# A retuned order for an attention and MoE kernel, a last chunk with one more float32 pair, and the softmax guard on another engine

## The chip, the cores and the metric

The kernel runs on one core of a Trainium2 chip. A core has five engines with a queue each, and every queue runs its instructions strictly in order: TensorE (PE; the profile shows its weight loads apart as PEld), VectorE (DVE), ScalarE (ACT), GpSimd (POOL) and SyncE (SP), which here only issues DMA transfers. Engines wait for each other by semaphores. The metric is the device time of the whole program in microseconds (us), the median of several runs.

## The reference

Two steps follow each other. The first is attention through 32 inducing points, done twice; the second is a feed-forward layer with a quadratic gate.

```
def mab(q, kv):
    s = scale * (q @ kv.transpose(0, 2, 1))
    s = s - s.max(-1, keepdims=True)
    a = np.exp(s)
    a /= a.sum(-1, keepdims=True) + 1e-09
    return a @ kv
h = mab(I, x)            # I [32, 128], x [4, 12480, 128] -> h [4, 32, 128]
attn = mab(x, h)         # [4, 12480, 128] = 49920 tokens
u = attn @ w_in          # [49920, 2048]
g = where(u >= 1, u, where(u <= -1, 0, (u + 1)**2 / 4))
out = g @ w_out          # [49920, 128]
```

The 1e-9 added to the softmax's sum is called the guard below.

## The kernel before

The four batches are cut into 26 chunks of 480 tokens each, 104 in all; four neighbouring chunks make a group (the last group of a batch has two). The feed-forward layer never forms the attention's output: it multiplies the attention weights (32 numbers per token) by hw = h @ w_in, so the hidden layer of a chunk comes from one matmul per 128 hidden columns. A chunk is worked in eight pairs k = 0 to 7, each of 256 hidden columns, that is two PSUM banks of 480 columns.

One pair goes like this. Two hidden matmuls on TensorE (L943) fill two of seven banks. ACT computes relu(u + 1) from the banks (L951), in one instruction of 960 columns where both banks are neighbours and taken together, else in two of 480, and squares it with a factor (L937). DVE takes the minimum of that and max(u, 1) (L956, 960 or twice 480 columns), which gives the gate g in a buffer w and frees the banks. Then g meets w_out. In the pairs of SPLIT = (0, 1, 3, 4, 6, 7) g is rounded to hi, a cast by DVE (L979), ACT (L976) or POOL (L974), and POOL forms lo = g - hi (L982); six matmuls (L1008) in the faster format add hi x w_lo, hi x w_hi and lo x w_hi. In the other pairs two float32 matmuls use g and w_f as they are (each shows as two records). The eight pairs add up in one bank; DVE transposes it (L1020) and four stores (L1024) write it out.

Beside the chunks of batch b run the steps that make ready what comes later. The summary of batch b + 1 (first attention) goes group by group: loads of x (L498), transposes on TensorE (L507), scores (L547), maximum (L552), exponential on ACT (L564), transposed weights copied to eN (L588, L596), weighted sums (L604, "the gather", copied by L611); then one chain over the groups: total maximum (L645 to L661), a rescaling exponential on ACT (L664), sums and reciprocals (L667 to L675), h (L678, L686, L690), and hw from h and w_in (L712, L717, L720, spread by DMAs, L732). The second attention of a group (`attend`) takes scores (L757), softmax steps on DVE, ACT and POOL (the guard on POOL, L783, the reciprocal on DVE, L786, the normalization on POOL, L789), and copies into aT by DMA (L823). For the very first chunk a shorter path (`attend_first`, L845 to L892) is taken.

At the start nothing can overlap: batch 0's summary, the weights (w_in and w_out are loaded and turned by L398 to L434 into exactly split parts; L463, L470 and L472 make the tiles w_f, w_lo and w_hi) and the first attention run before the first hidden matmul. In TensorE's gaps there the kernel puts warm-up matmuls of the identity (L1035, `keep_on`).

The order of all instructions is computed in Python when the kernel is built. Each step is added to a planner with an engine, a cost, a lag after which others can use its result, and a due time; a list scheduler then fixes the order of every engine. The due times come from a table DUE: one number per pair and kind of step (h hidden, r relu, s square, t the minimum, hi per engine, lo, p, pl and pf the matmuls), and further entries for the summary, the weights (wi, wc, wo, oc) and the start (names ending in 0). Five more numbers steer it: LONE (a price for taking two banks singly), WAIT, RETILE, RAW and WARM. So a number in this table changes an order and nothing else.

Of the kernel before, what the change touches and what calls it, by code (L numbers as in the profile page):

```python
# [9 lines left out]
F32 = mybir.dt.float32  # L10
# [8 lines left out]
AHEAD = []  # L19
# [28 lines left out]
    "end": [-102700],  # L48
# [15 lines left out]
LONE = {"r": 8650, "t": 0}  # L64
# [3 lines left out]
WAIT = 181850  # L68

RAW = dict(DVE=205, ACT=130, POOL=100, PE=100, SP=0)  # L70
RETILE = 100
# [174 lines left out]
def attn_moe(  # L246
# [127 lines left out]
    def load_f32(src, when, due, dst=None, after=None):  # L374
# [61 lines left out]
        f = add("SP", 1120, 3000, when, fetch, [after], [raw])  # L436
# [18 lines left out]
    def load_out(k, when, due):  # L455
        src = w_out[k * WS : (k + 1) * WS].rearrange("(p t) d -> p t d", t=2)
        whole, parted = any(k not in t for t in [SPLIT, *AHEAD]), any(k in t for t in [SPLIT, *AHEAD])
# [22 lines left out]
    def summarize(b, begin, pace, end):  # L480
# [610 lines left out]
```

## Time and profile before

| what | value |
|---|---|
| median of three runs | 1732.78 us (1732.76, 1732.78, 1734.93) |
| the profiled execution's own time | 1733.12 us |
| its span, from first to last instruction | 1731.2 us |
| mean granted TensorE clock | 0.996 |
| first hidden matmul (L943), first relu (L951) | 66.60, 67.12 us |
| end of the last matmul, of the span | 1725.28, 1731.2 us |
| busy: PE, DVE, ACT, POOL | 1702.3, 1625.2, 1662.0, 1619.2 us |

Busy time of PE counts pipelined matmuls with modelled ends. "w L951 <- PE banks L943" reads: ACT's instruction of line 951 that writes w waited for TensorE's of line 943 that writes banks. In rows by shape, "x976 | 531.6, 609" are instructions, busy us and mean ns of one, then follow the idle time ahead of them and what ended it. A PE instruction in float32 counts as two records.

### The profile page before, as it was taken

What the parts mean: (1) busy time and instruction counts of PE and PEld (TensorE: products, weight loads), DVE (VectorE), ACT (ScalarE), POOL (GpSimd) and SP (SyncE); (2) the same over time, 40 slices, a digit from 0 to 9 for tenths busy, and PEclk for the clock granted to TensorE, in tenths of its full rate; (3) what the DMA queues carried; (4) which work ended last, traced back from release to release, by engine and by line L of the source; (5) the groups of instructions that cost most, each with busy time, mean ns of one, the idle gap of its engine ahead of it and who ended that gap; (6) DMA issues with size and microseconds to landing.
All of it is one profiled execution on the core that took longest, in us unless ns stands there. A gap on an engine that the chain in (4) does not pass through costs nothing.

```text
span 1731.2 us, 26016 instructions
## 1 busy us (share of the span) xinstructions
PE 1702.3 (98%) x8100; PEld 1242.9 (72%) x8100; DVE 1625.2 (94%) x2123; ACT 1662.0 (96%) x2453; POOL 1619.2 (94%) x879
## 2 busy tenths in 40 slices
PE   7999999999999999999999999999999999999998
PEld 5777777777777777767767777777777777777776
DVE  4899999999999999999999999999999999999997
ACT  5699999999999999999999999999999999999997
POOL 1599999999899999999989999999999999999998
PEclk9899999999999999999999999999999999999999
DMA  8543334233343243342143333232212111111111
GB/s 210 136 75 69 67 60 81 48 63 62 62 83 60 51 79 65 64 80 56 36 85 63 73 65 71 51 66 52 44 27 59 35 31 29 34 35 35 34 30 18
DMA packets 427948, 105.74 MB, mean 61 GB/s; under 512 B 370562, under 2 KB 421218, under 8 KB 427810
## 3 DMA queue, kind: packets, MB, share of 16 engines
q1 hardware_dynamic: 427714, 103.96, 30.7%
q8 instruction: 64, 1.05, 0.3%
q14 instruction: 74, 0.61, 0.1%
q10 hardware_dynamic: 96, 0.13, 0.0%
HBM read 48.94 MB, written 25.56 MB: 43 GB/s over the span
## 4 chain that ended last, share of the span: by engine, by line
PE 72%; ACT 9%; DVE 8%; issue 4%; POOL 3%; DMA 2%; SPq 1%; POOLq 0%; DVEq 0%; ACTq 0%
PE banks L1008 49%; PE banks L943 16%; ACT w L951 5%; DVE w L956 4%; ACT w L937 4%; POOL lo L982 3%; DVE hi L979 2%; PE banks L604 1%; PE banks L757 1%; PE banks L547 1%; PE banks L507 1%; DMA xr<-in_x 1%; DVE oT L1020 1%; PE banks L588 1%; PE banks L1035 1%
## 5 line engine op out<-in xcount | busy, mean ns | idle before, releaser
L982 POOL TENSOR_TENSOR lo<-w,hi 128x960 fp32r<-128x960 f32 x624 | 1399.7, 2276 | 40.7 <-DVE hi L979 21.3
L956 DVE SCALAR_TENSOR_TENSOR w<-banks,w 128x480 f32<-128x480 f32 (+1 forms) x1158 | 957.0, 863 | 36.6 <-ACT w L937 30.2
L951 ACT ACTIVATE w<-banks 128x480 f32<-128x480 f32 (+1 forms) x1320 | 841.9, 711 | 16.6 <-PE banks L943 15.1
L937 ACT ACTIVATE w<-w 128x960 f32<-128x960 f32 x832 | 843.2, 1046 | 3.2
L943 PE MATMUL banks<-aT,hw 128*128 128x480 f32 x1664 | 592.3, 425 | 5.3 <-DVE w L956 3.1
L1008 PE MATMUL banks<-hi,w_lo 128*128 128x480 f32 x1248 | 520.6, 417 | 4.7 <-DVE oT L1020 3.6
L979 DVE TENSOR_REDUCE hi<-w 128x960 fp32r<-128x960 f32 x410 | 466.1, 1142 | 19.3 <-PE banks L1008 1.3
L1008 PE MATMUL banks<-hi,w_hi 128*128 128x480 f32 x1248 | 473.4, 379 | 0.0
L943 PEld LDWEIGHTS banks<-aT,hw 128*128 128x128 f32 x1664 | 305.6, 188 | 158.6 <-DVE w L956 74.0
L1008 PE MATMUL banks<-lo,w_hi 128*128 128x480 f32 x1248 | 398.8, 396 | 0.7 <-POOL lo L982 0.5
L1008 PE MATMUL banks<-w,w_f 128*128 128x480 f32 x832 | 395.3, 565 | 0.0
L1008 PEld LDWEIGHTS banks<-hi,w_lo 128*128 128x128 f32 x1248 | 234.8, 188 | 87.8 <-issue 26.4
L1008 PEld LDWEIGHTS banks<-lo,w_hi 128*128 128x128 f32 x1248 | 230.7, 188 | 73.6 <-issue 23.1
L1008 PEld LDWEIGHTS banks<-hi,w_hi 128*128 128x128 f32 x1248 | 234.7, 188 | 53.0 <-issue 22.0
L1008 PEld LDWEIGHTS banks<-w,w_f 128*128 128x128 f32 x832 | 156.1, 189 | 46.8 <-issue 27.2
L974 POOL TENSOR_SCALAR hi<-w 128x960 fp32r<-128x960 f32 x143 | 142.9, 1006 | 5.1 <-PE banks L943 1.2
L1020 DVE STREAM_TRANSPOSE oT<-banks 128x480 f32<-128x480 f32 x104 | 70.2, 675 | 9.9 <-PE banks L1008 9.5
L976 ACT CAST hi<-w 128x960 fp32r<-128x960 f32 x71 | 71.5, 1008 | 6.3 <-DVE w L956 2.3
L528 DVE STREAM_TRANSPOSE xT<-xr 128x480 f32<-128x480 f32 x78 | 51.2, 660 | 1.8 <-DMA xr<-in_x 1.8
L434 POOL TENSOR_TENSOR w_in_sb<-hi,lo 128x256 f32<-128x256 f32 x8 | 6.9, 862 | 39.8 <-DVE hi L423 39.8
L800 POOL TENSOR_TENSOR a<-a,ahi 128x480 fp32r<-128x480 f32 (+1 forms) x28 | 34.6, 1235 | 0.0
L552 DVE TENSOR_REDUCE mg<-banks 128x1 f32<-128x480 f32 (+1 forms) x28 | 18.1, 647 | 16.0 <-PE banks L547 16.0
(107 smaller groups left out, 609.7 us busy)
## 6 DMA issues: line engine op xcount, KB each, us to landing
out<-oT SPq DMA_DIRECT2D x416, 60.0 KB, 2.2
xn<-in_x SPq DMA_DIRECT2D x91, 240.0 KB, 4.4
xr<-in_x SPq DMA_DIRECT2D x312, 60.0 KB, 2.5
aT<-ahi SPq DMA_DIRECT2D x206, 60.0 KB, 2.0
aT<-a SPq DMA_DIRECT2D x206, 60.0 KB, 2.0
w<-in_moe_w_in SPq DMA_DIRECT2D x8, 256.0 KB, 3.6
w<-in_moe_w_out SPq DMA_DIRECT2D x8, 256.0 KB, 5.2
hw<-hy SPq DMA_DIRECT2D x32, 64.0 KB, 2.0
```

What stands on the lines that cost most here:

```text
L528: nc.vector.transpose(make(xT[b, c]), xr.tile.rearrange("c n i -> c (n i)"))
L800: nc.gpsimd.tensor_sub(a.tile.bitcast(F32R)[:rows], a.tile[:rows], a_hi.tile[:rows].bitcast(F32))
L937: nc.scalar.activation(w.tile, w.tile, AF.Square, scale=0.5)
L943: nc.tensor.matmul(make(h)[:, :CW], hw[b][ft // 4].tile[:, ft % 4 * P : (ft % 4 + 1) * P], aT[b, c].tile, start=True, stop=True,)
L951: each(of, i, hs_, w, lambda to, h: nc.scalar.activation(to, h, AF.Relu, bias=1.0))
L956: lambda to, h: nc.vector.scalar_tensor_tensor(to, h, 1.0, to, op0=ALU.max, op1=ALU.min),
L974: nc.gpsimd.tensor_scalar(make(hi), w.tile, 1.0, 0.0, op0=ALU.mult, op1=ALU.add)
L976: nc.scalar.copy(make(hi), w.tile)
L979: nc.vector.tensor_reduce(make(hi), w.tile.unsqueeze(3), axis=AX.X, op=ALU.max)
L982: nc.gpsimd.tensor_sub(make(lo), w.tile, hi.tile.bitcast(F32))
L1008: nc.tensor.matmul(acc.tile[:, :CW], wt[k][:, i, :], g.tile[:, i, :], start=first, stop=(acc.parts == 0),)
L1020: nc.vector.transpose(make(oT).rearrange("c n i -> c (n i)"), acc.tile[:, :CW])
```

## The change

Four edits, and a table.

1. The table DUE is replaced as a whole. Two new kinds stand in it: G and W give the time at which each of the seven groups of a summary begins, and at which its gather is due; before, both were equally spaced. LONE, WAIT and RETILE have other values, and the planner is told other costs and lags for the loads at the start (the weights' 1080 and 5500 ns for 1120 and 3000; x of batch 0: 1000 and 5800 for 1080 and 3000).
2. In the very last chunk the pairs of END = (0, 1, 3, 4, 6) are split; pair 7 stays in float32, which takes one more weight tile w_f7 (one ACT copy at the start), two more float32 matmuls and six fewer of the others, and one hi and one lo less.
3. The last chunk's four stores are issued by SP and ACT in turn, not all by SP.
4. The guard moves from POOL (L783 before) to DVE, right ahead of the reciprocal (L791, L792 after).

A branch for hi and lo taken from the banks is added too; its table KEPT is empty, so no pair takes it.

```diff
-AHEAD = []
+END = (0, 1, 3, 4, 6)
+KEPT = {}
...
-LONE = {"r": 8650, "t": 0}
+LONE = {"r": 20200, "t": 4100}
-WAIT = 181850
+WAIT = 173500
-RETILE = 100
+RETILE = 120
...
 DUE = {
...
+    "G": [-3000, 51380, 98260, 151290, 202220, 254700, 307980],
+    "W": [61076, 111606, 164336, 213966, 267096, 319426, 370406],
...
-        f = add("SP", 1120, 3000, when, fetch, [after], [raw])
+        f = add("SP", 1080, 5500, when, fetch, [after], [raw])
...
-                    "SP", 700 if b else 1080, 3000, at(due, "x") if b else at(0, "x0", c),
+                    "SP", 700 if b else 1000, 3000 if b else 5800, at(due, "x") if b else at(0, "x0", c),
...
         for g in range(NG):
-            load(g, begin + g * pace, pace * 0.2)
-            s = score(g, begin + (g + 0.85) * pace)
+            base = at(begin, "G", g)
+            load(g, base, pace * 0.2)
+            s = score(g, base + 0.85 * pace)
             if last:
-                gather(g - 1, begin + (g + 0.2) * pace, last)
+                gather(g - 1, at(begin, "W", g - 1), last)
...
-        def guard():
-            nc.gpsimd.tensor_scalar(sm[:rows], sm[:rows], 1e-9, None, op0=ALU.add)
-
         def invert():
+            nc.vector.tensor_scalar(sm[:rows], sm[:rows], 1e-9, None, op0=ALU.add)
             nc.vector.reciprocal(sm[:rows], sm[:rows])
...
-        o = add("POOL", 339, 440, AT[6], guard, [o], [s2])
-        o = add("DVE", 165, 300, AT[6], invert, [o], [s2])
+        o = add("DVE", 290, 430, AT[6], invert, [o], [s2])
...
+            split = k in (END if (b, c) == (B - 1, NCH - 1) else SPLIT)
+            kept = split and k in KEPT
...
-            if k in [*AHEAD, SPLIT][min(b * NCH + c, len(AHEAD))]:
+            if kept:
...
+            elif split:
...
-        def store(k):
+        def store(k, queue):
             ks = slice(k * M, (k + 1) * M)
-            nc.sync.dma_start(o_cols[b, c][:, :, ks], oT.tile[ks])
+            queue.dma_start(o_cols[b, c][:, :, ks], oT.tile[ks])
...
         for k in range(Q):
-            add("SP", 640, 3000, at(due, "o") + 5000, lambda k=k: store(k), [f], [oT])
+            engine = "ACT" if (b, c) == (B - 1, NCH - 1) and k % 2 else "SP"
+            add(engine, 640, 3000, at(due, "o") + 5000,
+                lambda k=k, queue=nc.scalar if engine == "ACT" else nc.sync: store(k, queue), [f], [oT])
```

Every line number after the change is some 5 to 8 higher in the first attention and some 40 higher at the end of a chunk (L951 becomes L958, L982 becomes L1024, L1035 becomes L1079).

What it does to the order, counted over the program: ACT has 1343 relu instructions for 1320 and 74 casts of hi for 71, and three eN copies fewer; DVE has 1199 instructions of L956's kind for 1158, 406 hi copies for 410, three eN copies more and the 28 guards; POOL has 623 lo for 624 and no guard; the warm-ups on TensorE fall from 81 to 65, and behind the first hidden matmul from 45 to 19.

Three places. The first is ACT around the rescaling exponential of batch 0 (L664 before, L672 after; mg and nm are the groups' and the total maximum; L398 and L405 are the first step on a loaded weight; w_ numbers below 200 are loads). Before:

```order
L611 COPY hs_72<-banks_64 128x128
L596 COPY eN_161_823<-banks_64 96x4x64
L598 COPY eN_161_823<-banks_64 96x64
L398 ACTIVATE hi_162_830<-w_150_768 128x256
L664 ACTIVATE banks_64<-mg_70,nm_0_83 128x7
L611 COPY hs_72<-banks_64 64x128
L463 COPY w_f5_97<-hi_145_753 128x256
L398 ACTIVATE hi_174_884<-w_167_849 128x256
```

and after:

```order
L405 ACTIVATE hi_164_832<-w_146_740 128x256
L470 COPY w_f5_97<-hi_141_728 128x256
L571 ACTIVATE e1_167_849,sg_71<-banks_64,nb_0_5_79 128x480
L603 COPY eN_173_870<-banks_64 96x512
L605 COPY eN_173_870<-banks_64 96x128
L672 ACTIVATE banks_64<-mg_70,nm_0_83 128x7
L405 ACTIVATE hi_175_879<-w_158_800 128x256
L479 CAST w_hi1_90<-hi_159_803 128x256
L479 CAST w_hi4_95<-hi_164_832 128x256
L618 COPY hs_72<-banks_64 128x128
```

The rebias ahead of the exponential was that of the load w_150; now the rebias next to it, of the load w_158, stands behind the exponential, and the last long group's own exponential and eN copies stand ahead of it. On TensorE the short group's ten gathers (L611 from eN_157) now stand ahead of the scores of that long group (L554), where the long group's twenty stood behind the short group's scores.

The second place is DVE before the first L956 (L412, L418, L423 of a weight load are L419, L425, L430 after; L892, after it L897, finishes aT for the first chunk). Before:

```order
L418 TENSOR_SCALAR hi_184_923<-lo_193_973 128x256
L892 TENSOR_TENSOR aT_195_982<-banks_64,aT_195_982 64x480
L423 SCALAR_TENSOR_TENSOR hi_184_923<-w_173_882,hi_184_923 128x256
L406 TENSOR_SCALAR lo_197_999<-hi_189_954 128x256
L403 TENSOR_SCALAR hi_191_967<-hi_191_967 128x256
L412 SCALAR_TENSOR_TENSOR lo_197_999<-w_175_894,lo_197_999 128x256
L406 TENSOR_SCALAR lo_202_1015<-hi_191_967 128x256
L418 TENSOR_SCALAR hi_189_954<-lo_197_999 128x256
L763 STREAM_TRANSPOSE banks_64<-banks_64 128x480
L423 SCALAR_TENSOR_TENSOR hi_189_954<-w_175_894,hi_189_954 128x256
L769 TENSOR_REDUCE mx_0_104<-banks_64 128x15
L956 SCALAR_TENSOR_TENSOR w_200_1008<-banks_64,w_200_1008 128x960
```

and after:

```order
L425 TENSOR_SCALAR hi_183_938<-lo_185_954 128x256
L430 SCALAR_TENSOR_TENSOR hi_183_938<-w_166_845,hi_183_938 128x256
L897 TENSOR_TENSOR aT_196_1016<-banks_64,aT_196_1016 64x480
L771 STREAM_TRANSPOSE banks_64<-banks_64 128x480
L777 TENSOR_REDUCE mx_0_105<-banks_64 128x15
L963 SCALAR_TENSOR_TENSOR w_201_1036<-banks_64,w_201_1036 128x960
L780 TENSOR_TENSOR s2_211_1067<-banks_64,mx_0_105 128x480
L963 SCALAR_TENSOR_TENSOR w_208_1049<-banks_64,w_208_1049 128x960
L788 TENSOR_REDUCE sm_0_106<-s2_211_1067 128x15
L1021 TENSOR_REDUCE hi_220_1091<-w_208_1049 128x960
L791 TENSOR_SCALAR sm_0_106<-sm_0_106 128x15
L792 RECIPROCAL sm_0_106<-sm_0_106 128x15
```

Ten weight operations stood behind L892, between the first steps of the second attention and the first chunk's gate or after it; now all stand ahead of L897. POOL and ACT show the same: six POOL operations (L431, L470) and three ACT casts (L472) that stood behind the first relu are ahead of it. The last row but one is the guard in its new place.

The third place is the end of TensorE's queue (lo and hi are the two parts of g; w_f7 is the new tile, w the gate itself). Before:

```order
L1008 MATMUL banks_64<-lo_4755_16589,w_hi4_95 128x480 x2
L1008 MATMUL banks_64<-w_4745_16544,w_f5_97 128x480
L1008 MATMUL banks_64<-hi_4756_16600,w_lo7_101 128x480
L1008 MATMUL banks_64<-hi_4756_16600,w_hi7_100 128x480
L1008 MATMUL banks_64<-hi_4756_16600,w_lo7_101 128x480
L1008 MATMUL banks_64<-hi_4756_16600,w_hi7_100 128x480
L1008 MATMUL banks_64<-hi_4754_16587,w_lo6_99 128x480
L1008 MATMUL banks_64<-hi_4754_16587,w_hi6_98 128x480
L1008 MATMUL banks_64<-hi_4754_16587,w_lo6_99 128x480
L1008 MATMUL banks_64<-hi_4754_16587,w_hi6_98 128x480
L1008 MATMUL banks_64<-lo_4757_16602,w_hi6_98 128x480 x2
L1008 MATMUL banks_64<-lo_4758_16611,w_hi7_100 128x480 x2
```

and after:

```order
L1050 MATMUL banks_64<-hi_4750_16612,w_lo4_96 128x480
L1050 MATMUL banks_64<-hi_4750_16612,w_hi4_95 128x480
L1050 MATMUL banks_64<-hi_4750_16612,w_lo4_96 128x480
L1050 MATMUL banks_64<-hi_4750_16612,w_hi4_95 128x480
L1050 MATMUL banks_64<-w_4753_16623,w_f7_100 128x480 x2
L1050 MATMUL banks_64<-lo_4754_16633,w_hi4_95 128x480 x2
L1050 MATMUL banks_64<-w_4746_16595,w_f5_97 128x480 x2
L1050 MATMUL banks_64<-hi_4755_16643,w_lo6_99 128x480
L1050 MATMUL banks_64<-hi_4755_16643,w_hi6_98 128x480
L1050 MATMUL banks_64<-hi_4755_16643,w_lo6_99 128x480
L1050 MATMUL banks_64<-hi_4755_16643,w_hi6_98 128x480
L1050 MATMUL banks_64<-lo_4756_16649,w_hi6_98 128x480 x2
```

Pair 7's six matmuls with hi and lo are gone, and two with w_f7 stand between pair 4's hi and lo. Behind these rows DVE's transpose and the four stores are the same but for the stores' queues.

More of the change, by code (lines that the diff above doesn't have):

```diff
@@ L30 @@
 DUE = {
[17 rows of a table removed]
-    "end": [-102700],
[11 rows of a table removed]
[17 rows of a table added]
+    "end": [-103350],
[15 rows of a table added]
 }
 WARM = (28000, 180)
-LONE = {"r": 8650, "t": 0}
+LONE = {"r": 20200, "t": 4100}
 KEEP = 0
-WAIT = 181850
+WAIT = 173500
 RAW = dict(DVE=205, ACT=130, POOL=100, PE=100, SP=0)
-RETILE = 100
+RETILE = 120
 class Slot:
@@ L456, in load_out @@
         src = w_out[k * WS : (k + 1) * WS].rearrange("(p t) d -> p t d", t=2)
-        whole, parted = any(k not in t for t in [SPLIT, *AHEAD]), any(k in t for t in [SPLIT, *AHEAD])
+        whole, parted = any(k not in t for t in [SPLIT, END]), any(k in t for t in [SPLIT, END])
         by = lambda a: a.rearrange("p (t c) -> p t c", t=2)
@@ L626, in summarize @@
         for g in range(NG):
-            load(g, begin + g * pace, pace * 0.2)
-            s = score(g, begin + (g + 0.85) * pace)
+            base = at(begin, "G", g)
+            load(g, base, pace * 0.2)
+            s = score(g, base + 0.85 * pace)
             if last:
-                gather(g - 1, begin + (g + 0.2) * pace, last)
+                gather(g - 1, at(begin, "W", g - 1), last)
             last = s
-        gather(NG - 1, begin + (NG + 0.2) * pace, last)
+        gather(NG - 1, at(begin, "W", NG - 1), last)
         m1 = small("m1", [P, 1], f"_{b}")
@@ L912, in half, with each @@
         return int(hs_[i].place > hs_[1 - i].place)
-    def each(of, i, hs_, w, do):
+    def each(of, i, hs_, do, *ws):
         if of[1 - i].wide:
@@ L919, in each @@
             a, b = sorted(h.place for h in hs_)
-            do(w.tile, banks[:, a : b + 1, :CW])
+            do(banks[:, a : b + 1, :CW], *(w.tile for w in ws))
         else:
-            do(w.tile[:, half(i, hs_)], hs_[i].tile[:, :CW])
+            do(hs_[i].tile[:, :CW], *(w.tile[:, half(i, hs_)] for w in ws))
     def chunk(b, c):
@@ L933, in chunk @@
             hs_ = [h0, in_turn("h", h0)]
-            ms, rs_, ts = [], [], []
+            ms, rs_, ts, us, ls = [], [], [], [], []
+            split = k in (END if (b, c) == (B - 1, NCH - 1) else SPLIT)
+            kept = split and k in KEPT
             def square(w=w):
@@ L950, in rise, with bound @@
                         make(w)
-                    each(of, i, hs_, w, lambda to, h: nc.scalar.activation(to, h, AF.Relu, bias=1.0))
-                def bound(i=i, w=w, hs_=hs_, of=ts):
+                    each(of, i, hs_, lambda h, to: nc.scalar.activation(to, h, AF.Relu, bias=1.0), w)
+                def bound(i=i, w=w, hs_=hs_, of=ts, kept=kept):
                     each(
-                        of, i, hs_, w,
-                        lambda to, h: nc.vector.scalar_tensor_tensor(to, h, 1.0, to, op0=ALU.max, op1=ALU.min),
+                        of, i, hs_,
+                        lambda h, t: nc.vector.scalar_tensor_tensor(
+                            h if kept else t, h, 1.0, t, op0=ALU.max, op1=ALU.min
+                        ), w,
                     )
@@ L967, in chunk, with upper, lower @@
             plan.twins(*ts, 1070, 1200, LONE["t"])
-            if k in [*AHEAD, SPLIT][min(b * NCH + c, len(AHEAD))]:
+            if kept:
+                hi, lo = in_turn("hi"), in_turn("lo")
+                for i, h in enumerate(hs_):
+                    def upper(k=k, i=i, hi=hi, hs_=hs_, of=us):
+                        if hi.tile is None:
+                            make(hi)
+                        if KEPT[k] == "ACT":
+                            each(of, i, hs_, lambda h, to: nc.scalar.copy(to, h), hi)
+                        else:
+                            each(
+                                of, i, hs_, lambda h, to: nc.vector.tensor_reduce(
+                                    to, h.unsqueeze(len(h.shape)), axis=AX.X, op=ALU.max
+                                ), hi,
+                            )
+                    def lower(i=i, hi=hi, lo=lo, hs_=hs_, of=ls):
+                        if lo.tile is None:
+                            make(lo)
+                        each(of, i, hs_, lambda h, u, to: nc.vector.tensor_sub(to, h, u.bitcast(F32)), hi, lo)
+                    cost, both = (457, 868) if KEPT[k] == "ACT" else (568, 1070)
+                    us.append(add(KEPT[k], cost, cost + 138, at(due, "xh", k) + i, upper, [ts[i]], [h, hi]))
+                    ms.append(lower)
+                plan.twins(*us, both, both + 130, LONE["t"])
+                for i, h in enumerate(hs_):
+                    ls.append(add("DVE", 568, 700, at(due, "xl", k) + i, ms[2 + i], [us[i]], [h, hi, lo]))
+                plan.twins(*ls, 1070, 1200, LONE["t"])
+                parts = [
+                    ([(w_lo, hi), (w_hi, hi)], 436, "p", us, [hi]),
+                    ([(w_hi, lo)], 218, "pl", ls, [lo]),
+                ]
+            elif split:
                 hi, lo = in_turn("hi"), in_turn("lo")
```

58 rows, old and new, of the table DUE are left out of this document.

## The prediction

> **What bounds the kernel now.** I read the page's totals first, then a table by stage, then what ScalarE (ACT) waits for, and last the order in time of the start and the end. The totals:
>
> ```profile
> PE 1702.3 (98%) x8100; PEld 1242.9 (72%) x8100; DVE 1625.2 (94%) x2123; ACT 1662.0 (96%) x2453; POOL 1619.2 (94%) x879
> ```
>
> All four engines are nearly full over the whole span, which tells little, so the table by stage comes next. Its columns are the stretch, its length, then busy time and instructions of PE, PEld, DVE, ACT and POOL, the granted TensorE clock, the DMA share and GB/s.
>
> ```profile
> 47.50:50.90 3.40, 2.17 (x34) 1.69 (x32) 1.36 (x8) 1.93 (x8) 1.36 (x2) 1.00 1.09 240
> 50.90:61.20 10.30, 10.19 (x51) 8.27 (x52) 6.19 (x22) 2.29 (x7) 2.30 (x3) 0.50 0.72 187
> 61.20:66.60 5.40, 5.40 (x52) 5.40 (x50) 4.91 (x17) 2.21 (x6) 1.96 (x3) 1.00 0.42 101
> 66.60:100.00 33.40, 31.94 (x190) 24.46 (x189) 31.93 (x50) 29.72 (x45) 28.28 (x22) 1.00 0.43 82
> 100.00:1700.00 1600.00, 1591.26 (x7218) 1157.41 (x7217) 1536.75 (x1934) 1578.82 (x2296) 1553.52 (x825) 1.00 0.29 56
> ```
>
> In the body (100 to 1700 us) ACT is busy 1578.82 of 1600 us, 98.7%; DVE 96%, POOL 97%. PE's 99% counts overlapped matmuls and is no proof. So ACT bounds the body, with at most 21.2 us to win there, and everything before ACT's first relu (67 us) and after its last square is a serial stretch. What ACT waits for once the relus run, and what holds TensorE's weight loads in the body (columns: us in total, times, longest):
>
> ```profile
> ACT w L951 <- PE banks L943: 15.1, 30, 1.1
> PEld banks L943 <- DVE w L956: 72.0, 215, 1.0
> ```
>
> The second row is the coupling behind the first: a hidden matmul (L943) waits for a bank that DVE's L956 has not emptied, 72.0 us in all, and 15.1 us of it, 21%, reaches ACT as a missing bank. DVE lateness is passed on at about a fifth.
>
> **The change, part by part.** Work first, from the rows by shape (busy us, mean ns):
>
> ```profile
> L956 DVE SCALAR_TENSOR_TENSOR w<-banks,w 128x960 f32<-128x960 f32 x506 | 569.6, 1145 | 27.4 <-ACT w L937 23.0 <-POOL hi L974 2.1 <-issue 0.4
> L951 ACT ACTIVATE w<-banks 128x480 f32<-128x480 f32 x976 | 531.6, 609 | 15.8 <-PE banks L943 14.7
> L979 DVE TENSOR_REDUCE hi<-w 128x960 fp32r<-128x960 f32 x410 | 466.1, 1142 | 19.3 <-PE banks L1008 1.3 <-DVE w L956 0.5 <-POOL lo L982 0.3
> L956 DVE SCALAR_TENSOR_TENSOR w<-banks,w 128x480 f32<-128x480 f32 x652 | 395.5, 645 | 9.2 <-ACT w L937 7.3
> L951 ACT ACTIVATE w<-banks 128x960 f32<-128x960 f32 x344 | 339.8, 1001 | 0.8 <-PE banks L943 0.4
> L976 ACT CAST hi<-w 128x960 fp32r<-128x960 f32 x71 | 71.5, 1008 | 6.3 <-DVE w L956 2.3 <-PE banks L1008 2.1 <-POOL w_lo L470 0.8
> L596 ACT COPY eN<-banks 120x512 f32<-120x512 f32 x12 | 7.7, 642 | 0.0
> L783 POOL TENSOR_SCALAR sm<-sm 128x15 f32<-128x15 f32 x24 | 6.2, 260 | 2.0
> ```
>
> ACT. The new order has 1343 relu instructions for 1320: 23 pairs that were one 960-wide relu become two of 480. Busy time per instruction is 531.6/976 = 0.545 and 339.8/344 = 0.988 us, so 23 x (2 x 0.545 - 0.988) = +2.3 us. Three more casts of hi on ACT (74 for 71) add 3 x 1.007 = +3.0; three eN copies that go to DVE give back 3 x 0.64 = -1.9. Three weight casts (w_hi, 0.41 us each in the row at 68.09 below) now stand ahead of the first relu: -1.2. ACT's body: **+2.2 us**, paid in full, since ACT is the bound.
>
> DVE. 41 more pairs are taken in halves: 41 x (2 x 395.5/652 - 569.6/506) = +3.6. Four fewer hi copies: 4 x 1.137 = -4.5. Three eN copies: about +2.0. The 28 guards: an L869 of 128x4, the nearest row (below), took 0.16, so 28 x 0.16 = +4.5. Together +5.6 us on an engine with 63 us idle in the body; at the fifth found above, **+1.1 us** arrives at ACT. POOL loses 28 guards (7.2 us) and one lo (2.24), 9.5 us in all; it has 46 us idle and is named as what ACT waited for only in single cases, so this is worth nothing by itself.
>
> The start. Rows in order of time (start, duration, idle before and its releaser):
>
> ```profile
> 46.10 0.14 DVE L645 TENSOR_REDUCE m<-mg 128x1 f32<-128x7 f32 x1
> 46.29 0.66 ACT L564 ACTIVATE e<-banks,nb 64x480 f32<-64x480 f32 x1 [1.29 <-DVE m L645]
> 49.43 0.27 PE L604 MATMUL banks<-xn,eN 96*32 96x128 f32 x1
> 49.94 0.43 ACT L398 ACTIVATE hi<-w 128x256 f32<-128x256 f32 x1 [1.45 <-DMA w<-in_moe_w_out]
> 50.27 0.25 ACT L664 ACTIVATE banks<-mg,nm 128x7 f32<-128x7 f32 x1
> 51.47 2.48 PE L1035 MATMUL banks<-ident 128*128 128x128 f32 x10
> 53.74 3.03 PE L686 MATMUL banks<-ff,hs 128*128 128x32 f32 x14
> 57.72 0.66 PE L845 MATMUL banks<-xT,hT 128*32 128x128 f32 x8
> 58.15 1.94 PE L712 MATMUL banks<-w_in_sb,hT 128*32 128x512 f32 x8
> 60.01 4.37 PE L1035 MATMUL banks<-ident 128*128 128x128 f32 x32
> 66.60 0.71 PE L943 MATMUL banks<-aT,hw 128*128 128x480 f32 x2
> 68.09 0.41 ACT L472 CAST w_hi<-hi 128x256 fp32r<-128x256 f32 x1
> ```
>
> From the last maximum (L645, 46.10) to the first hidden matmul (66.60) are 20.5 us, one chain. Two things in it are avoidable. ACT stood 1.45 us behind a w_out load before it could do L664, the next step of the chain; in the new order the rebias of a late load (L405) stands behind that step, so -1.4. And the stage table has the clock at 0.50 from 50.9 to 61.2: the five warm-up matmuls (2.48 us, of which about 1.0 delays L686), L686 (3.03), L845 and L712 (2.6 together) and the two warm-ups before them (0.7 of delay) ran at half speed. At full clock they would lose half of 3.03 + 2.6 = 2.8, and the 1.0 and 0.7 with it: -4.5. The second block of warm-ups shrinks from 16 to 13 (32 records in 4.37 us), and L883 stood behind it: -0.9. Against this, TensorE now scores the longest-delayed group only after the short group's whole gather. That stretch took 3.4 us here (46.29 to 49.70), with four scores more some 3.9: **+3.9**. Sum -1.4 - 4.5 - 0.9 + 3.9 = **-2.9 us** (ends -6.8, nothing late; and +3.9, no gain).
>
> The ramp behind it. The weights' last preparation ran among the first relus (10 DVE, 6 POOL, 3 ACT instructions); ACT lost 33.4 - 29.7 = 3.7 us there, 0.5 of it ahead of the first relu:
>
> ```profile
> 71.38 0.40 ACT L472 CAST w_hi<-hi 128x256 fp32r<-128x256 f32 x1 [0.66 <-POOL hi L431]
> 85.98 1.00 ACT L976 CAST hi<-w 128x960 fp32r<-128x960 f32 x1 [0.81 <-POOL w_lo L470]
> ```
>
> In the new order all of that preparation stands ahead of the first relu on all three engines. At the body's rate (21.2 idle in 1600) the stretch would idle 0.4 us, so 3.2 - 0.4: **-2.8** (ends -3.2 and 0). The cover is DVE's idle time beside the chain: it is busy 6.19 of 10.3 and 4.91 of 5.4 us there, 4.6 us free for the ten operations (at 0.28 to some 0.4, by the row at 65.18 below: 3.5 us); what does not fit comes back as a later start.
>
> The end.
>
> ```profile
> 1715.67 8.87 POOL L982 TENSOR_TENSOR lo<-w,hi 128x960 fp32r<-128x960 f32 x4
> 1717.21 1.00 ACT L937 ACTIVATE w<-w 128x960 f32<-128x960 f32 x1
> 1719.71 0.97 PE L1008 MATMUL banks<-w,w_f 128*128 128x480 f32 x2
> 1724.59 0.69 PE L1008 MATMUL banks<-lo,w_hi 128*128 128x480 f32 x2 [0.51 <-POOL lo L982]
> 1725.32 0.68 DVE L1020 STREAM_TRANSPOSE oT<-banks 128x480 f32<-128x480 f32 x1 [5.33 <-PE banks L1008]
> L1024 SPq DMA_DIRECT2D out<-oT x10: 569/624/627, 1699.5 to 1728.0; - x10
> ```
>
> Four stores follow each other on SP at 0.624 us; two on each of two queues save 2 x 0.624 = **-1.25 us**. Before them POOL's four lo in a row (8.87 us) release the last matmuls. Pair 7 kept in float32 takes one away (2.22), but TensorE must do two more float32 matmuls (one is the 0.97 row; overlapped, some 1.6 us for both). From the end of the last square (1718.21) to the transpose (1725.32) were 7.1 us; now two halves on DVE (1.2), a hi (1.0), a lo (2.24), its two matmuls (0.7) and the 1.6 between make 6.7: **-0.4** (ends -2.2, a whole lo, and +0.5).
>
> The retuned table itself moves nearly every row of the body. Nothing in the trace prices that; I take 0 (ends -8 and +8, half of ACT's waits each way).
>
> Sum: +2.2 + 1.1 - 2.9 - 2.8 - 1.25 - 0.4 = -4.05 from the profiled execution's 1733.12, which is 0.34 above the median (1732.78): **1728.7**.
>
> **The rivals.**
>
> *The clock halves again.* The half-speed stretch began right after 47.5 to 50.9, where PE was busy 2.17 of 3.40 us, and the new order has the same waits on single-column steps there. Without the 4.5 us the start costs +1.6: 1728.7 + 4.5 = 1733.2, no change. For it: the waits stay. Against: more warm-ups stand in the gaps before L656. The Trainium skill ("TensorE: Matmul & The Clock Gate", Part 1) has the clock fall to exactly half after an idle window and the windows run free of the program; by that rule this case is as open as I leave it, and 0.50 and 1.00 agree with it.
>
> *Guards stall on DVE: slower.* In the trace a small DVE operation that overlaps a running POOL one can end only with it:
>
> ```profile
> 61.82 0.16 DVE L869 TENSOR_SCALAR sm_first<-sm_first 128x4 f32<-128x4 f32 x1
> 64.27 0.84 POOL L431 TENSOR_TENSOR hi<-hi,lo 128x256 f32<-128x256 f32 x1 [0.76 <-DVE hi L423]
> 64.45 0.81 DVE L403 TENSOR_SCALAR hi<-hi 128x256 f32<-128x256 f32 x1
> 65.18 0.28 DVE L418 TENSOR_SCALAR hi<-lo 128x256 uint32<-128x256 uint32 x1
> ```
>
> L403 needed 0.81 until just after POOL's L431 ended; its like at 65.18, alone, 0.28. A guard of the same operation that meets a running lo (2.24 us, POOL 97% busy) would wait 1.1 us on average: 28 x 1.1 = 31 us on DVE, which has 63 idle. At the fifth it passes on 6; if half arrives at ACT, 1728.7 + 15 = 1744. It decides from 7.5 us arriving (1736.2). For it: those rows. Against: DVE's idle time, and 28 stalls are one in four chunks. The Trainium skill ("SBUF — State Buffer", Who interferes with whom) gives VectorE and GpSimd one shared pair of ports, locked for a whole instruction, and lists tensor_scalar among those that take it; L403's rows agree, and no row here shows it for 15 columns.
>
> *The new order also closes body gaps.* Half of ACT's 21.2 us goes: 1728.7 - 10 = 1719. For it: the 15.1 us of waits on banks; against: more split pairs.
>
> *It does not do what it says.* The hi/lo branch on banks is switched by an empty table and never runs; if the start is no earlier and the extra float32 pair holds TensorE at the end, the stores alone count against the 3.3 us of work on ACT and DVE: 1732.78 + 3.3 - 1.25, about 1734.8.
>
> **How the numbers follow.** Forecast case 0.35 (its own range 1725 to 1733), clock again half 0.24, guards 0.14, body gaps 0.17, stores alone 0.10. About 0.2%, 3.5 us, is what a measurement here can tell from no change: faster means under 1729.3. Faster: 0.6 x 0.35 + 0.15 x 0.24 + 0.17 = 0.42. Slower (over 1736.2): 0.13 of the guards, 0.04 of the clock case with a late start, 0.05 of the others: 0.22. Same: 0.36. Range 1719 to 1740, which takes in the body-gap case and the guards up to 11 us.
>
> **What would show it.** First hidden matmul at 63.7 and the clock at 1.00 from 50 to 62 (clock case: 0.50 again, about 68). ACT idle in the 33 us after it under 2 us. Guards L791: 0.16 each, or a spread up to 2.3 with L795's chain later. ACT's idle time from 100 to 1700 near 21 us; last store's start about 1.2 us after the first. Wrong if ACT's idle time in the body moves by over 5 us, or if the first relu stands anywhere outside 62 to 69.

## The result and the profile after

The changed kernel takes 1750.45 us (median of four runs, 1749.09 to 1752.46) where the kernel before takes 1732.77: 1.0104 times as long, 95% interval 1.0086 to 1.0122. It is 17.7 us slower. The profiled execution took 1750.04 us, its span is 1748.1. One execution of run 4 below took 7528.2 us and is left out of that run's figures. The totals of the page:

```profile
span 1748.1 us, 25941 instructions
PE 1704.6 (98%) x8066; PEld 1229.2 (70%) x8066; DVE 1647.6 (94%) x2191; ACT 1671.0 (96%) x2477; POOL 1611.1 (92%) x850
```

As before, the shares say little: DVE and ACT are 94% and 96% busy of a longer span. Cut at three points, the two profiles differ like this (first relu, end of the last square and the last transpose are rows of the timeline):

| stretch | before | after | difference |
|---|---|---|---|
| start to first relu | 67.1 | 69.5 | +2.4 |
| first relu to end of last square ("body" from here on) | 1651.1 | 1666.4 | +15.3 |
| last square to the transpose | 7.1 | 6.9 | -0.2 |
| transpose to the end | 5.9 | 5.3 | -0.6 |

So the loss lies in the body. The table by stage for the changed kernel, with the same columns as in the prediction:

```profile
47.50:50.90 3.40, 3.40 (x51) 2.84 (x43) 2.29 (x10) 1.83 (x6) 2.57 (x2) 1.00 0.60 150
50.90:61.20 10.30, 9.03 (x109) 7.28 (x102) 9.77 (x30) 5.45 (x16) 4.45 (x7) 1.00 0.55 150
61.20:66.60 5.40, 5.24 (x51) 4.21 (x51) 4.91 (x16) 1.45 (x5) 1.49 (x2) 1.00 0.11 28
66.60:100.00 33.40, 32.30 (x166) 22.92 (x165) 27.75 (x41) 30.93 (x45) 26.07 (x17) 1.00 0.49 94
100.00:1700.00 1600.00, 1579.48 (x7140) 1138.27 (x7139) 1542.49 (x1979) 1568.14 (x2292) 1530.41 (x791) 1.00 0.29 55
```

The clock stays at 1.00 through the start. In the 1600 us of the body ACT is busy 1568.14 us where it was 1578.82, so its idle time grew from 21 to 32 us; DVE is the only one of ACT, DVE, POOL and TensorE that is busier (1542.49 for 1536.75). What ACT waits for and what holds TensorE's weight loads (us, times, longest):

```profile
ACT w L958 <- PE banks L950: 20.0, 40, 1.6
PEld banks L950 <- DVE w L963: 85.9, 209, 2.2
```

The two rows of the prediction again (15.1 and 72.0 before): both rose, and the longest wait for a bank that DVE had not emptied went from 1.0 to 2.2 us. The longest guard lasts as long, as the rows of the one new DVE instruction show (min, median and max in ns, first and last start):

```profile
L791 DVE TENSOR_SCALAR sm<-sm x28: 132/764/2227, 76.5 to 1658.8; 128x15 f32<-128x15 f32 x24, 64x15 f32<-64x15 f32 x4
...
147.17 2.28 POOL L1024 TENSOR_TENSOR lo<-w,hi 128x960 fp32r<-128x960 f32 x1
147.49 1.99 DVE L791 TENSOR_SCALAR sm<-sm 128x15 f32<-128x15 f32 x1
152.41 0.57 ACT L958 ACTIVATE w<-banks 128x480 f32<-128x480 f32 x1 [0.56 <-PE banks L950]
406.40 0.15 DVE L791 TENSOR_SCALAR sm<-sm 64x15 f32<-64x15 f32 x1
406.81 2.28 POOL L1024 TENSOR_TENSOR lo<-w,hi 128x960 fp32r<-128x960 f32 x1 [0.75 <-ACT w L944]
```

At 147.49 POOL had just begun a lo; the guard, 15 numbers per partition, ended at 149.48, POOL's lo at 149.45. Three us later ACT missed a bank for 0.56 us. At 406.40 POOL was idle until 406.81: 0.15 us. In all, 18 of the 28 guards end 0.02 to 0.04 us after a row of POOL ends, and the three that met an idle POOL took 0.15; the other seven fell into rows that merge several POOL instructions. By the groups of rows, the 28 guards took 24.4 + 2.7 = 27.1 us on DVE, 0.97 us each.

### The profile page after: what moved, and what is told of

The parts are those of the page before. It is cut to its first block, busy times and chain, and to the rows that moved or that the text cites. A ratio compares the mean times of both kernels' runs of the same rounds, so it can differ in the third digit from the quotient of the medians.

```text
span 1748.1 us, 25941 instructions
## 1 busy us (share of the span) xinstructions
PE 1704.6 (98%) x8066; PEld 1229.2 (70%) x8066; DVE 1647.6 (94%) x2191; ACT 1671.0 (96%) x2477; POOL 1611.1 (92%) x850
## 5 line engine op out<-in xcount | busy, mean ns | idle before, releaser
L1024 POOL TENSOR_TENSOR lo<-w,hi 128x960 fp32r<-128x960 f32 x623 | 1396.8, 2270 | 50.6 <-DVE hi L1021 25.1
L963 DVE SCALAR_TENSOR_TENSOR w<-banks,w 128x480 f32<-128x480 f32 (+1 forms) x1199 | 957.2, 837 | 38.4 <-ACT w L944 35.7
L958 ACT ACTIVATE w<-banks 128x480 f32<-128x480 f32 (+1 forms) x1343 | 839.8, 691 | 22.3 <-PE banks L950 20.0
L944 ACT ACTIVATE w<-w 128x960 f32<-128x960 f32 x832 | 834.7, 1034 | 3.2
L1021 DVE TENSOR_REDUCE hi<-w 128x960 fp32r<-128x960 f32 x406 | 460.9, 1140 | 14.0
L1050 PE MATMUL banks<-lo,w_hi 128*128 128x480 f32 x1246 | 391.8, 392 | 0.9 <-POOL lo L1024 0.8
L1050 PEld LDWEIGHTS banks<-hi,w_hi 128*128 128x128 f32 x1246 | 234.5, 188 | 53.4 <-issue 22.9
L795 POOL TENSOR_TENSOR s<-s,sm 128x480 f32<-128x480 f32 (+1 forms) x28 | 27.9, 995 | 8.0 <-DVE sm L792 6.3
```

The costliest lines, as they stand in the source:

```text
L944: nc.scalar.activation(w.tile, w.tile, AF.Square, scale=0.5)
L958: each(of, i, hs_, lambda h, to: nc.scalar.activation(to, h, AF.Relu, bias=1.0), w)
L963: lambda h, t: nc.vector.scalar_tensor_tensor(h if kept else t, h, 1.0, t, op0=ALU.max, op1=ALU.min), w,
L1021: nc.vector.tensor_reduce(make(hi), w.tile.unsqueeze(3), axis=AX.X, op=ALU.max)
L1024: nc.gpsimd.tensor_sub(make(lo), w.tile, hi.tile.bitcast(F32))
L1050: nc.tensor.matmul(acc.tile[:, :CW], wt[k][:, i, :], g.tile[:, i, :], start=first, stop=(acc.parts == 0),)
```

## The experiments

Four theories stood against each other: G, the guards' stalls on DVE made the body longer; O, the new order did; and, once G was clear, D and L on how DVE's lost time reaches the end. Most runs keep an order row for row and change only what one step issues, because a step that is added to the planner or priced anew gives another order (with one price altered, run 7, the changed kernel has 25985 instructions for 25941). Ratios are to the kernel before on the same chip.

**1. No guard.** The changed kernel's order; the addition is left out.

```diff
-            nc.vector.tensor_scalar(sm[:rows], sm[:rows], 1e-9, None, op0=ALU.add)
             nc.vector.reciprocal(sm[:rows], sm[:rows])
```

> The changed kernel without the guard: the 28 additions of 1e-9 are left out, and nothing else; every engine's order is that of the changed kernel. In the changed kernel the 28 guards on DVE lasted 27.1 us together. If their stalls are what made the body longer (theory G), this comes back to about 1736 us and ACT's body idle falls by some 7 us or more. If the new order itself did it (theory O), it stays at 1748 to 1750. If DVE's lateness is passed on at the fifth that was estimated before, 27 x 0.21 = 5.7 us come back: 1744 to 1745.

1733.92 us, 1.0004 (0.9995 to 1.0014). The guards cost 16.5 us, 61% of their 27.1 us; theory G. The body is 1649.1 us, 17.3 less than with them. In the same views:

```profile
ACT w L958 <- PE banks L950: 8.8, 19, 1.0
...
PEld banks L950 <- DVE w L963: 65.0, 198, 1.1
...
100.00:1700.00 1600.00, 1590.16 (x7205) 1152.60 (x7205) 1534.97 (x1977) 1580.65 (x2319) 1546.97 (x799) 1.00 0.29 56
```

ACT's waits for banks fall from 20.0 to 8.8 us and its busy time in the 1600 us rises to 1580.65. The whole body, in the columns of the table by stage, of the kernel before, the changed kernel and this run:

```profile
67.12:1718.21 1651.09, 1640.88 (x7477) 1195.21 (x7476) 1585.33 (x2003) 1626.69 (x2365) 1599.43 (x855) 1.00 0.29 56
...
69.51:1735.94 1666.43, 1644.56 (x7424) 1185.25 (x7424) 1604.23 (x2062) 1633.69 (x2385) 1589.92 (x822) 1.00 0.29 55
...
73.90:1723.01 1649.11, 1638.15 (x7424) 1187.55 (x7424) 1579.90 (x2034) 1628.89 (x2385) 1589.36 (x821) 1.00 0.29 56
```

ACT's idle time in the body is 24.4, 32.7 and 20.2 us. So 12.5 of the 17.3 us that the guards add are idle time of ACT. The other 4.8 us are busy time of the same 2385 instructions (1633.69 for 1628.89); why they take longer is not settled.

**2. The guard back on POOL, in the new order.**

```diff
-            nc.vector.tensor_scalar(sm[:rows], sm[:rows], 1e-9, None, op0=ALU.add)
+            nc.gpsimd.tensor_scalar(sm[:rows], sm[:rows], 1e-9, None, op0=ALU.add)
```

> The changed kernel's order, with the guard issued by POOL at the same place of the program (0.26 us each by the row of before). G: near the kernel without a guard, about 1736 to 1738. O: 1748 to 1750. At a fifth: 1744 to 1746. The guards on POOL should last 0.26 each, whatever runs on DVE.

1763.69 us, 1.0176 (1.0157 to 1.0194): slower still, and no theory had that. The guards do last 0.26 each, but now DVE's in-order queue stands at the reciprocal until POOL has finished what is ahead of the guard:

```profile
DVE sm L792 <- POOL sm L791: 35.6, 25, 2.6
```

35.6 us of waiting in 25 places. An order made for a guard on DVE leaves no time for the way over POOL. In the order before, the reciprocal shows no such wait: there DVE's queue has other work between the sum and the reciprocal.

**3. The guard on DVE, in the old order.**

```diff
         def guard():
-            nc.gpsimd.tensor_scalar(sm[:rows], sm[:rows], 1e-9, None, op0=ALU.add)
+            pass
         def invert():
+            nc.vector.tensor_scalar(sm[:rows], sm[:rows], 1e-9, None, op0=ALU.add)
```

> The old order of every engine, with only the guard moved from POOL to DVE, right ahead of its reciprocal. G: the guards stall on running POOL operations as in the changed kernel (0.7 to 1.0 us on average) and cost 10 to 15 us: 1743 to 1748. O: 1733 to 1735. At a fifth: about 1738.

1752.13 us, 1.0115 (1.0100 to 1.0130): +18.8 us in the order before, with nothing else changed, and more than any theory had. So the loss is the guard's in either order.

```profile
L786 DVE TENSOR_SCALAR sm<-sm x28: 132/480/2226, 77.5 to 1662.7; 128x15 f32<-128x15 f32 x24, 64x15 f32<-64x15 f32 x4
```

23.3 us of guards by the groups of rows (21.6 + 1.7), body 1669.9, 18.8 more than before and 17.6 more than in run 6, which has the old order without a guard.

**4. The stores on two queues, in the old order.**

```diff
-            nc.sync.dma_start(o_cols[b, c][:, :, ks], oT.tile[ks])
+            queue = nc.scalar if (b, c) == (B - 1, NCH - 1) and k % 2 else nc.sync
+            queue.dma_start(o_cols[b, c][:, :, ks], oT.tile[ks])
```

> The old order with only the last chunk's four stores taken in turn by SP and ACT. The span's last 5.9 us (from the start of the last transpose to the end) should lose 2 x 0.624 = 1.25 us if the issue time is what they wait for, 0.6 us (as the changed kernel shows: 5.3 us) if the second queue's first transfer is slower to issue or to land. Total 1731.5 to 1732.2 us; guard and order theories say nothing here.

1732.73 us, 0.9997 (0.9986 to 1.0009): no change that the times can show. The forecast for this run was 1731.5 to 1732.2. In the profile the stretch from the transpose to the end is 5.3 us for 5.9, as in the changed kernel. The changed kernel's rows there (ns):

```profile
L1066 SPq DMA_DIRECT2D out<-oT x2: 569/598/626, 1743.5 to 1744.1; - x2
L1066 ACTq DMA_DIRECT2D out<-oT x2: 662/737/812, 1743.5 to 1744.2; - x2
```

From the transpose's start (1742.79) to the last issue are 1.4 us, where 2.7 were (1725.32 to 1728.0): the predicted 1.25 us went. From the last issue to the end are 3.9 us where 3.2 were, so 0.7 came back: the last issue takes 0.81 us on ACT's queue where it took 0.63 on SP's, and from issue to landing are up to 2.8 us where the four stores before had at most 2.2.

**5. Another operation in the guard's place.** A maximum over one element, which changes no number.

```diff
-            nc.vector.tensor_scalar(sm[:rows], sm[:rows], 1e-9, None, op0=ALU.add)
+            nc.vector.tensor_reduce(sm[:rows], sm[:rows].unsqueeze(2), axis=AX.X, op=ALU.max)
```

> The changed kernel's order, with the 28 guards replaced on DVE by a tensor_reduce of the same 128x15 onto itself (a maximum over one element each, which changes no number; the addition of 1e-9 is left out). Same instruction count, same waits, another operation. If an extra DVE instruction in this place costs as such (its length and the step in the chain), most of the guard's 16.5 us stay: over 1743. If it is the operation, held up by POOL, each one lasts about 0.15 us and the time is that without a guard plus 28 x 0.15 x 0.8: 1734 to 1738.

1733.99 us, 1.0009 (1.0000 to 1.0018), as without any instruction there.

```profile
L791 DVE TENSOR_REDUCE sm<-sm x28: 128/157/160, 76.0 to 1643.1; 128x15 f32<-128x15 f32 x24, 64x15 f32<-64x15 f32 x4
```

Same place, same size, same wait on the sum, and never over 0.16 us beside the same POOL instructions. So the operation matters: DVE's place in the chain is not what holds it up.

**6. The old order without a guard**, and the last stores on two queues.

```diff
         def guard():
-            nc.gpsimd.tensor_scalar(sm[:rows], sm[:rows], 1e-9, None, op0=ALU.add)
+            pass
```

> The old order without the guard on either engine (the addition of 1e-9 is left out), and the last four stores on two queues. POOL loses 28 x 0.26 = 7.2 us and the attention chain two hand-overs per group. If POOL's time counts as DVE's does (some 0.7 us per us), 1727; if POOL's idle time covers it, 1732 to 1733, the stores' 0.6 us alone. Beside the changed kernel without a guard it also gives the two orders' own difference: the bodies of the profiles were 1649.1 there and 1651.1 in the kernel before.

1733.15 us, 1.0001 (0.9992 to 1.0011). POOL's 7.2 us of guards were worth nothing that the times can show. Against the fifth run (guardless, new order) the body is 1652.3 for 1649.4, the first relu at 65.8 for 69.0: the new order's body is 2.9 us shorter and its start 3.1 us longer, and the two cancel. These are single profiles: the kernel before and run 4, with the same order in the body, differ by 1.8 us there (1651.1 and 1652.9).

**7. The right price in the planner.**

```diff
-        o = add("DVE", 290, 430, AT[6], invert, [o], [s2])
+        o = add("DVE", 1220, 1360, AT[6], invert, [o], [s2])
```

> The changed kernel, guard on DVE, but the planner is told 1220 ns for guard and reciprocal instead of 290 (what they took: 0.97 + 0.25 us); the order follows from that. If the loss is a plan made with a wrong price, a good part of 16.5 us comes back: under 1744. If the stall cannot be planned away (DVE's time is simply used), it stays at 1748 to 1752.

1753.22 us, 1.0117 (1.0102 to 1.0132), above both ranges. The guards still took 26.0 us (22.6 + 3.4), one of them 3.0 us, and the body is 1669.3. Knowing the price did not help. As the order is another one too, the run does not say what the price alone does.

**8. The new table with the old start.** Entries wi, wc, wo, oc, A0, e0, x0, t0, s0, g0 and the loads' costs as before; no guard.

> The new table without a guard, but with the old due times and costs for all that runs before the first relu (loads, weights, batch 0's summary and first attention). The order of the body follows and is not that of the changed kernel. If the new start is what costs (first relu at 69.5 where the kernel before has 67.1) and the body's table is neutral or better, 1730 to 1732; if the body's order is as accidental as its due times, it may land anywhere from 1730 to 1742, with the first relu at 66 to 67.5 in either case.

1756.56 us, 1.0134 (1.0118 to 1.0150), without a single guard. The first relu came at 70.7, not earlier, and the body took 1674.4. It fell outside all that was expected, and what costs the 25 us in this order's body is not settled. Parts of two tables that each give 1733 us can give 1757, so this mixture says nothing of what the new start is worth.

**9 and 10. One and two more sums in the guard's place**, which POOL cannot hold up.

```diff
-            nc.vector.tensor_scalar(sm[:rows], sm[:rows], 1e-9, None, op0=ALU.add)
+            nc.vector.tensor_reduce(sm[:rows], s2.tile[:rows], axis=AX.X, op=ALU.add)   # once, or twice
```

> The changed kernel's order, with the guard's place taken by a second run of the sum before it (L788's tensor_reduce, 128x480, 0.64 us each, 0.56 after overlap; the addition of 1e-9 is left out): 16 us more on DVE that no POOL instruction can hold up. Against the kernel with a 128x15 reduction there (1734.0, 4.4 us more on DVE, nothing paid), theory D says that DVE's time passes on at the guard's rate, 16.5 of 27 us, so +10: 1742 to 1746. Theory L says it is the length of a single stall that counts (a block of 0.56 us is caught by the seven banks, one of 1.5 to 2.2 is not): 1734 to 1737.

> As the run with one more sum, with two more in the guard's place: 31 us more on DVE in blocks of 1.1 us, a little more than the guards took (27.1). D: 31 x 0.61 = 19 us over the kernel without a guard, 1750 to 1756. L: clearly less than the guards' 16.5, under 1745.

One more: 1736.29 us, 1.0025 (1.0015 to 1.0034). Two more: 1756.23 us, 1.0141 (1.0124 to 1.0157). Sixteen us on DVE cost 2.4, 31 cost 22. L is wrong with its "under 1745" for the second, D with its 1742 for the first. The stage rows, 100 to 1700 us, of the first and the second:

```profile
100.00:1700.00 1600.00, 1589.87 (x7192) 1148.29 (x7191) 1544.03 (x1998) 1577.94 (x2315) 1542.54 (x797) 1.00 0.29 55
...
100.00:1700.00 1600.00, 1578.06 (x7119) 1133.69 (x7118) 1543.11 (x1999) 1564.31 (x2285) 1524.89 (x789) 1.00 0.29 55
```

DVE's busy time stops at 1543 to 1544 us of 1600, the same as in the changed kernel (1542.49), where run 1 has 1534.97: in this order more work on DVE from there on made the span longer and DVE no fuller.

**11. The guard kept on DVE as an addition of a tile.**

```diff
+        nc.vector.memset(eps, 1e-9)
-            nc.vector.tensor_scalar(sm[:rows], sm[:rows], 1e-9, None, op0=ALU.add)
+            nc.vector.tensor_add(sm[:rows], sm[:rows], eps[:rows])
```

> The changed kernel's order and result, with the guard on DVE as an addition of a constant 128x15 tile of 1e-9 (tensor_tensor with two inputs from SBUF) for the addition of a number. If POOL holds up only the tensor_scalar form, each takes 0.15 to 0.2 us and the time is 1734 to 1736, the guard kept. If a second input from SBUF waits for POOL too, the stalls are those of the changed kernel, 0.5 to 1.0 us on average, and the time 1746 to 1751.

1749.17 us, 1.0101 (1.0086 to 1.0116), as the changed kernel.

```profile
L793 DVE TENSOR_TENSOR sm<-sm,eps 128x15 f32<-128x15 f32 x24 | 24.3, 1013 | 0.0
```

1013 ns each for the guard's 1018: the form with two inputs from SBUF is held up just as the tensor_scalar is. The Trainium skill ("SBUF — State Buffer", Who interferes with whom) says both: a tensor_scalar in a two-port mode contends with GpSimd for a shared pair of ports, a VectorE instruction with two inputs from SBUF contends with a GpSimd instruction that reads SBUF, and on trn2 tensor_reduce never contends. The three rows (means of 1018 and 1013 ns, median of 157 ns) agree.

**12 and 13. The same DVE time in two blocks per group; in half of the groups.**

```diff
# 12
-            nc.vector.tensor_scalar(sm[:rows], sm[:rows], 1e-9, None, op0=ALU.add)
+            nc.vector.tensor_reduce(sm[:rows], s2.tile[:rows], axis=AX.X, op=ALU.add)
...
             nc.vector.transpose(make(a)[:rows], s2.tile[:rows].rearrange("p n m -> p (n m)"))
+            nc.vector.transpose(a.tile[:rows], s2.tile[:rows].rearrange("p n m -> p (n m)"))
# 13
-            nc.vector.tensor_scalar(sm[:rows], sm[:rows], 1e-9, None, op0=ALU.add)
+            for _ in range(2 if g % 2 == 0 else 0):
+                nc.vector.tensor_reduce(sm[:rows], s2.tile[:rows], axis=AX.X, op=ALU.add)
```

> The changed kernel's order without the guard; per group one more sum in the guard's place (0.56 us) and the transpose back (L800, 128x480, some 0.6 us) run twice: as much more DVE time as the run with two more sums (32 us), in two separate blocks. The runs so far fit 'DVE absorbs some 0.4 us of it per group and the rest is paid in full' (0.16 x 28: 0 paid; 0.56 x 28: 3.9; 0.97 x 28: 17.3; 1.12 x 28: 23.0, from the bodies). If what is absorbed is a fixed amount per group, or DVE's time is simply full, this costs 28 x (1.16 - 0.4) = 21: 1752 to 1757. If it is per block, because the seven banks catch one short delay and recover before the next, 28 x (0.16 + 0.2) = 10 or less: 1737 to 1745.

> The changed kernel's order without the guard; two more sums (1.12 us) in 16 of the 28 groups, none in the others: 18 us in all, near the 16 of one more sum in every group (1736.3). If DVE has some 11 us to give over the whole program, 18 - 11 = 7 are paid: 1740 to 1742. If it absorbs about 0.4 us of each block, 16 x 0.72 = 11.5 are paid: 1744 to 1747. If time in all counts, 1736 to 1738 as with one more sum in every group.

Two blocks: 1753.82 us, 1.0117 (1.0100 to 1.0134); half of the groups: 1747.29 us, 1.0079 (1.0063 to 1.0095). The same excess in two separate blocks is paid like one block, so no limit per block; 18 us in 16 groups cost much more than 16 us in 28, so no budget over the whole program either. What fits is a limit per group. In the table the DVE time added per group is by the rows (starts of one sum to the next 0.56, the second transpose some 0.6), and the cost is the body's, over the 1649.1 without a guard:

| run | added per group, us | body, us | cost per group with it, us | not paid, us |
|---|---|---|---|---|
| 5, small reduction | 0.16 x 28 | 1649.4 | 0.01 | 0.15 |
| 9, one sum | 0.56 x 28 | 1653.1 | 0.14 | 0.42 |
| changed kernel, guard | 0.97 x 28 | 1666.4 | 0.62 | 0.35 |
| 10, two sums | 1.12 x 28 | 1672.1 | 0.82 | 0.30 |
| 12, sum and transpose | 1.16 x 28 | 1671.2 | 0.79 | 0.37 |
| 13, two sums | 1.12 x 16 | 1663.8 | 0.92 | 0.20 |

Of the DVE time added to a group of four chunks 0.2 to 0.4 us vanish (the 0.16 of run 5 wholly); the rest is paid in full. In the old order run 3 over run 6 fits as well: 23.3 us added, 17.6 paid, 0.20 per group not paid. Each row is one profile, and the 1.8 us between two profiles of one order are 0.06 per group. Why that is so is argued, not shown: ACT has to make up for what it missed, and without a guard its idle time in the body is 20.2 us, 0.7 per group, while TensorE's loads wait 65.0 us for banks from DVE even then, so the banks hold little reserve for a late DVE. Of DVE's own idle time, 69.2 us, 40.4 are waits of L963 for ACT's squares.

No version here beats the kernel before. The changed kernel without its guard equals it. Since the maximum is subtracted first, each sum holds one exp(0) = 1, and in float32 1 + 1e-9 is 1, so nothing is lost with the addition.

## Why the prediction was wrong

The forecast was 1728.7, range 1719 to 1740; measured 1750.45. The rival that happened is the one with the guards stalling on DVE, placed and priced at "28 x 1.1 = 31 us on DVE"; 27.1 were measured. Both signs of being wrong came: ACT's idle time from 100 to 1700 us moved by 10.7 us (21.2 to 31.9), and the first relu stood at 69.5. Term by term:

**The guard: the step that failed.** Two choices in it. First, the price: the sum took "the nearest row", an L869 of 0.16 us at a moment when POOL was idle, for an engine that meets a POOL busy 97% of the time. The row for that condition was L403's (0.81 beside a running L431), and it stood in the prediction, under a rival with a chance of 0.14. In place of 4.5 us on DVE there were 27.1. Second, the rate: "DVE lateness is passed on at about a fifth". That was one total of waits (15.1) over another (72.0), which says how the waits of a steady state divide, not what a further delay costs. Measured was 17.3 of 27.1 us in the new order, 17.6 of 23.3 in the old one (run 3 over run 6), and nothing of 4.4 (run 5): a small free part per group, then one for one. With what the guards cost put in, the sum is 1728.7 - 1.1 + 17 = 1745; the rest is mostly the start.

**The start: wrong by 5.3 us.** Predicted -2.9, measured +2.4. The first relu is later in every profile of this start: 69.5 here, 68.9 to 70.1 in runs 2, 5 and 9 to 13, and 73.9 in run 1, where the old order's runs 3, 4 and 6 have 67.0, 66.3 and 65.8.

```profile
47.60 0.66 ACT L571 ACTIVATE e<-banks,nb 64x480 f32<-64x480 f32 x1 [1.04 <-PE banks L611]
50.72 0.98 PE L554 MATMUL banks<-xT,indT 128*32 128x480 f32 x6
51.66 0.91 DVE L419 SCALAR_TENSOR_TENSOR lo<-w,lo 128x256 uint32<-128x256 uint32 x1
52.61 0.29 DVE L425 TENSOR_SCALAR hi<-lo 128x256 uint32<-128x256 uint32 x1
52.82 0.65 DVE L559 TENSOR_REDUCE mg<-banks 128x1 f32<-128x480 f32 x1
53.79 0.15 DVE L653 TENSOR_REDUCE m<-mg 128x1 f32<-128x7 f32 x1
55.88 0.28 ACT L672 ACTIVATE banks<-mg,nm 128x7 f32<-128x7 f32 x1
59.74 1.75 PE L694 MATMUL banks<-ff,hs 128*128 128x32 f32 x14 [0.63 <-DVE ff L686]
62.64 1.04 PE L720 MATMUL banks<-w_in_sb,hT 128*32 128x512 f32 x8
63.62 3.17 PE L1079 MATMUL banks<-ident 128*128 128x128 f32 x26
68.99 0.70 PE L950 MATMUL banks<-aT,hw 128*128 128x480 f32 x2
```

Two terms were mis-sized. The first is the +3.9 for the stretch from the short group's exponential (L571) to the last maximum (L653). It took 6.19 us, and 6.17 to 6.19 in all the runs that keep this start. TensorE's part came nearly as priced: the long group's scores (L554) ended at 51.70, 4.1 us after the exponential began. But the term stops there. Two weight operations (L419, L425) stood ahead on DVE's queue, then came the long group's own maximum (L559) and two small steps: 2.1 us more.

The second is the gain behind the maximum. From there to the first hidden matmul are 15.2 us where 20.5 were, 5.3 less and not 6.8. The rescaling exponential (L672, L664 before) comes 2.1 us after the maximum where it came 4.2 after it: -2.1, for -1.4. From that exponential to the first hidden matmul are 13.1 us for 16.3: -3.2, where the clock and the shorter warm-ups had -5.4. The remaining 1.5 us is how far the short group's exponential started behind the earlier maximum (46.10 to 47.60). Most of that is no property of the order: this exponential began at 46.3 to 48.3 us in the old order's profiles and at 45.8 to 50.4 in the new order's.

The clock stayed at 1.00 in this execution, but not in every one of this order: in the profiles of runs 1 and 11 it was at half for 3.4 us, and the stretch from the exponential L672 to the first hidden matmul took 14.8 and 14.7 us for 13.1, some 1.6 more. In the old order, runs 3, 4 and 6 had 3.4 us at half where the kernel before had 10.2, and the same stretch took 15.3, 15.8 and 15.0 us for 16.3: 6.8 us less of half speed were worth 0.5 to 1.3. By these rows the 4.5 for all of it was too much, but no profile shows the old order at full clock throughout.

**The ramp: right.** Predicted -2.8. The 33.4 us from the first relu on, before:

```profile
67.10:100.50 33.40, 31.94 (x188) 24.30 (x187) 31.93 (x51) 30.17 (x46) 28.30 (x23) 1.00 0.44 83
```

and after:

```profile
69.50:102.90 33.40, 31.56 (x151) 21.98 (x151) 29.57 (x41) 32.75 (x46) 26.84 (x17) 1.00 0.49 90
```

ACT idles 0.65 us for 3.23: -2.6. The same 33.4 us in runs 1 and 5 have 0.64, in the old order's runs 4 and 6 3.15 and 3.14.

**ACT's work: right.** Predicted +2.2. ACT is busy for 1626.69 us of the body before and 1628.89 without a guard in the new order (run 1): +2.2; run 5 over run 6 gives +1.0. **POOL's 9.5 us: right** at nothing (run 6). **The end**: predicted -1.25 for the stores and -0.4 for the float32 pair; measured -0.6 and -0.2. The issue time went as said; the missing term was what the second queue's issue and landing take longer, 0.7 us. **The table's body order**, taken as 0: outside the ramp ACT idles 19.6 and 20.7 us in the new order without a stall (runs 1 and 5), and 21.2, 22.1 and 22.9 in the old one (the kernel before, runs 6 and 4). That is some 2 us to the good, little more than two profiles of one order differ.

The numbers of the part on what would show it: ACT idle after the first relu under 2 us came true. The clock was at 1.00 from 50 to 62, but the first hidden matmul came at 68.99 and not at 63.7. "Guards L791: 0.16 each, or a spread up to 2.3" was the right sign to look for, and its second half came (132 to 2227 ns).

## What to carry to other kernels

Price an instruction that is moved to another engine under the conditions that it will meet there: which of the other engines' instructions run at that time, and whether a row of the trace shows it beside one of those. A total of waits divided by another is not a rate at which a new delay passes on. On engines that wait for each other in turn, idle time need not be a reserve: here a delay beyond a few tenths of a us per group was paid in full. And an order computed for one placement of the work belongs to it: the same 28 additions put back on POOL cost 30 us in the order that was made without them.

## What the runs showed of the hardware

A DVE tensor_scalar or two-input tensor_tensor of 15 columns, 0.15 us beside an idle POOL, took up to 2.2 us beside a busy one, 1.0 us on average, and ended with a POOL instruction; one in run 7 took 3.0 us, longer than one of POOL's lo (2.3). A tensor_reduce of the same size in the same place took 0.157 us (run 5). The reciprocal right behind it took 0.20 to 0.25 in all runs. Half clock on TensorE for 3.4 us of the start cost 1.6 us in the new order (runs 1 and 11); 6.8 us of it less in the old order gained 0.5 to 1.3 (runs 3, 4 and 6). A DMA issue took 0.66 and 0.81 us on ACT's queue, 0.57 and 0.63 on SP's.
